# Attention and gated MLP on one core: 64-bit weights made into float32 in place, with other staging and schedule numbers

## The chip, the cores and the metric

The kernel runs on one NeuronCore of one Trainium2 chip. The time is the device time of one execution in microseconds (us); the median of a few runs is compared. The engines named below are PE (matrix products; PEld is its weight load, which overlaps), DVE (vector), ACT (scalar, activations), POOL (general purpose) and SP, which here only issues the DMA transfers. Each engine works through its own instructions strictly in the order in which they were emitted.

## The reference

A causal attention with two kinds of sparse masks (heads 0 to 3 see the last 32 keys, heads 4 to 7 see each 32nd key), then a gated MLP whose gate mixes the 576 positions by a 576x576 matrix:

```python
# B, H, S, D = 8, 8, 576, 64; d_model 512; d_ff 1024
def _attn_ref(q, k, v):
    scores = scale * np.matmul(q, k.transpose(0, 1, 3, 2))
    scores = np.where(masks[None, :, :, :], scores, -1000000000.0)
    scores = scores - np.max(scores, axis=-1, keepdims=True)
    attn = np.exp(scores)
    attn = attn / (np.sum(attn, axis=-1, keepdims=True) + 1e-09)
    return np.matmul(attn, v).astype(np.float32)

def _moe_ref(x, w_in, w_spatial, b_spatial, w_out):
    h = np.maximum(x @ w_in, 0.0)
    u, v = (h[..., :d_ff // 2], h[..., d_ff // 2:])
    mu = np.mean(v, axis=-1, keepdims=True)
    var = np.mean((v - mu) ** 2, axis=-1, keepdims=True)
    v_n = (v - mu) / np.sqrt(var + 1e-06)
    v_s = np.einsum('ts,bsd->btd', w_spatial, v_n) + b_spatial[None, :, None]
    return ((u * v_s) @ w_out).astype(np.float32)
```

`w_in` (512x1024) and `w_out` (512x512) come as 64-bit floats: the input code multiplies a float32 array by a 64-bit scalar. All else is float32.

## The kernel before

**Products.** Every large product is made of three: an operand is split into a rounded part ("0", type fp32r) and the rest ("1"), and the pairs (0,0), (0,1), (1,0) of `PROD` are summed in PSUM. `rnd` makes the rounded part (ACT, DVE or POOL), `rest` the difference (DVE or POOL).

**Stages.** Attention runs per batch and pair of heads `t` (32 of them, four to a batch): scores on PE (L387 local, L497 strided, tiles `s`), masks and maxima (L407 on DVE for local ones; L512 to L525 for strided ones), the exponential on ACT (L424, L530), `normalise` (L360 to L369), a 32x32 transpose on DVE into `pc` (L440, L547), copies of its blocks into `ptl` or `pts` (`rnd`, L318/L320), the products with v (L469, L563, tiles `po`), and the split into `x` (L337 or L339, then L328). The MLP has `moe_1` for a batch (v half L764, u half L806, the mean and variance chain L727 to L751, the split into `vn`), `moe_tail` for the last 64 positions of each batch (same lines, tiles with 64 partitions; its results are `tail` and `tail_b`), and `moe_2`: the spatial product L886 with its last part L898/L899 from the tail, the gate L908, the split into `g`, and the projection L928, whose result goes out through `o`.

**Weights.** Before the first batch can go through the MLP, `weight` has to turn twelve tiles of 128x512 64-bit values (512 KB each) into the two float32 parts: four for the u half of `w_in`, four for its v half, four for `w_out`. A tile is loaded as pairs of 32-bit words into a slot of the rings `u` or `g` (which the MLP itself uses later), two slots each. Then: DVE masks the exponent out of the upper word (L639) into a temporary; ACT turns it into a power of two (L646); DVE extracts the mantissa's upper bits (L652), adds the lower word (L656), POOL or DVE multiplies by the power of two (L660), DVE puts the sign on (L663), and `rnd` and `rest` make the two parts. The temporaries stand in the rings `xt` and `tail`.

**Order.** No order is written out. `Program` collects the operations with what they read and write, a duration on each engine that can do them, and a key; `order` goes through them as a list scheduler would (an idle engine takes the ready operation of the lowest key; an operation with several engines goes to the one that the durations say is done first), and the instructions are emitted in that order. The table `KEYS` holds keys of the first eight attention pairs ("a"), of the weights ("v", "u", "o"), of the spatial weights ("s", "t"), how far ahead attention runs ("lead"), a penalty on DVE ("dp") up to a time ("dpt"), keys of the memsets ("fill") and how far PE looks for a small tiled product beside another ("near"). `warm` puts small products on zeros (L1053) into gaps of PE.

Of the kernel before, what the change touches and what calls it, by code (L numbers as in the profile page):

```python
# [12 lines left out]
U32 = mybir.dt.uint32  # L13
# [66 lines left out]
class Fixed:  # L80
    """A tile that stays; called for it like a Buf."""
# [8 lines left out]
class Buf:  # L90
    """One use of a slot of a ring; its tile is taken from the pool when it is first emitted."""
# [28 lines left out]
class Program:  # L120
    """Operations with what they read and write, put in an issue order for each engine by
    list scheduling: an idle engine takes the ready operation of the lowest key."""

    def __init__(self):
        self.ops, self.writer, self.readers, self.spare = [], {}, {}, {}
        self.tiled = set()

    def add(self, key, choices, fn, reads=(), writes=(), spare=None, tiled=False):
        n = len(self.ops)
        if spare is not None:  # L130
# [23 lines left out]
    def order(self):  # L154
# [12 lines left out]
        issued = []  # L167

# [13 lines left out]
        while len(issued) < len(ops):  # L182
# [45 lines left out]
            taken[n] = True  # L228
            free[e] = now + cost
# [30 lines left out]
def pe_cost(m, n):  # L260
    return max(m / 1.2, n / 2.4 + 3.0)
# [3 lines left out]
def attention_moe(ctx, tc, qT, kT, vl, vs, cst, w_in, w_out, wsp, wtail, out):  # L265
    nc = tc.nc
    nb = qT.shape[0]
    wide = w_in.dtype != F32
# [44 lines left out]
    def rnd(key, n, dst, src, reads, writes, engs=(ACT, DVE, POOL)):  # L313
# [816 lines left out]
```

## Time and profile before

| | |
|---|---|
| runs shown | 564.25, 564.97 (median), 565.13 us |
| span of the profiled execution, first to last instruction | 562.7 us (the page names no other time for it) |
| PE, share of the span | 94% |
| DVE | 64% |
| ACT | 42% |
| POOL | 23% |
| DMA, mean rate over the span | 93 GB/s |
| granted TensorE clock, mean | 0.982 |

How to read it: the shares are averages over two different regimes. The first 100 us make the weights and the attention of the first two batches; the rest is the MLP of eight batches with the attention of the next ones beside it. A row of a group reads: line, engine, operation, output<-inputs, shapes, count | busy us, mean ns of one | idle time before it and what ended most of it. "Busy" counts an instruction from its start to its end, so that two that overlap in the pipe are counted once in a window.

### The profile page before, as it was taken

What the parts mean: (1) busy time and instruction counts of PE and PEld (TensorE: products, weight loads), DVE (VectorE), ACT (ScalarE), POOL (GpSimd) and SP (SyncE); (2) the same over time, 40 slices, a digit from 0 to 9 for tenths busy, and PEclk for the clock granted to TensorE, in tenths of its full rate; (3) what the DMA queues carried; (4) which work ended last, traced back from release to release, by engine and by line L of the source; (5) the groups of instructions that cost most, each with busy time, mean ns of one, the idle gap of its engine ahead of it and who ended that gap; (6) DMA issues with size and microseconds to landing.
All of it is one profiled execution on the core that took longest, in us unless ns stands there. A gap on an engine that the chain in (4) does not pass through costs nothing.

```text
span 562.7 us, 13842 instructions
## 1 busy us (share of the span) xinstructions
PE 529.5 (94%) x5550; PEld 489.4 (87%) x5550; DVE 361.5 (64%) x1090; ACT 236.1 (42%) x733; POOL 129.8 (23%) x200
## 2 busy tenths in 40 slices
PE   7787796899999999999999999999999999999997
PEld 7655676897988989999799989899899989998997
DVE  5799899948488456566836774994645662535232
ACT  7757564714374135333634354571353233212211
POOL 4777987401112022000220121200101010001000
PEclk8999897799999999999999999999999999999999
DMA  7876451416045103035303340461031100010011
GB/s 239 259 226 197 149 205 30 135 44 182 1 144 164 60 24 98 5 120 166 100 1 102 131 129 5 148 183 55 2 104 38 61 31 1 20 46 21 1 43 44
DMA packets 26352, 52.28 MB, mean 93 GB/s; under 512 B 3376, under 2 KB 11696, under 8 KB 26288
## 3 DMA queue, kind: packets, MB, share of 16 engines
q1 hardware_dynamic: 26288, 51.39, 29.8%
q8 instruction: 44, 0.72, 0.6%
q14 instruction: 20, 0.16, 0.1%
HBM read 41.94 MB, written 9.44 MB: 91 GB/s over the span
## 4 chain that ended last, share of the span: by engine, by line
PE 68%; DVE 19%; POOL 4%; ACT 4%; DMA 2%; issue 2%; SPq 0%; POOLq 0%; ACTq 0%; DVEq 0%
PE m L928 17%; PE m L806 15%; PE m L886 14%; PE m L764 13%; ACT pl L424 2%; DVE x L328 2%; PE po L469 2%; POOL ptl L320 2%; PE po L563 2%; PE m L898 1%; PE s L387 1%; PE m L899 1%; DVE bn L732 1%; DVE tail L656 1%; DMA kbd<-kT 1%
## 5 line engine op out<-in xcount | busy, mean ns | idle before, releaser
L886 PE MATMUL m<-wsp_sb,vn 128*128 128x288 f32 x768 | 114.4, 300 | 3.5 <-POOL wsp_sb L328 1.5
L886 PEld LDWEIGHTS m<-wsp_sb,vn 128*128 128x128 f32 x768 | 107.7, 192 | 5.4 <-POOL wsp_sb L328 2.1
L928 PE MATMUL m<-g,w_out_sb 128*128 128x288 f32 x768 | 107.1, 297 | 0.1
L806 PE MATMUL m<-x,w_in_sb 128*128 128x288 f32 x768 | 106.4, 298 | 0.2 <-ACT vv L727 0.2
L806 PEld LDWEIGHTS m<-x,w_in_sb 128*128 128x128 f32 x768 | 104.4, 190 | 1.6 <-ACT vv L727 0.4
L928 PEld LDWEIGHTS m<-g,w_out_sb 128*128 128x128 f32 x768 | 103.5, 188 | 1.5 <-issue 0.8
L764 PE MATMUL m<-w_in_sb,x 128*128 128x512 f32 (+1 forms) x408 | 99.0, 398 | 0.7 <-POOL w_in_sb L328 0.6
L764 PEld LDWEIGHTS m<-w_in_sb,x 128*128 128x128 f32 (+1 forms) x408 | 74.3, 185 | 20.5 <-POOL w_in_sb L328 1.0
L337 ACT COPY o<-m 128x288 f32<-128x288 f32 x55 | 21.9, 399 | 114.4 <-PE m L928 96.6
L908 DVE TENSOR_TENSOR u<-m,u 128x288 f32<-128x288 f32 x64 | 28.4, 454 | 54.5 <-PE m L899 54.1
L328 DVE TENSOR_TENSOR x<-po,x 128x288 fp32r<-128x288 f32 x64 | 35.4, 571 | 39.0 <-ACT x L337 38.5
L744 POOL TENSOR_TENSOR bn<-bn,sel 128x1 f32<-128x1 f32 (+1 forms) x37 | 22.4, 606 | 157.3 <-DVE bn L740 155.5
L424 ACT ACTIVATE pl<-pl,ml 128x64 f32<-128x64 f32 (+1 forms) x160 | 53.6, 337 | 5.5 <-DVE ml L407 5.3
L732 DVE BATCH_NORM_STATS2 bn<-vv 128x6 f32<-128x512 f32 (+1 forms) x37 | 25.4, 687 | 42.0 <-ACT vv L727 41.7
L820 ACT ACTIVATE u<-m 128x288 f32<-128x288 f32 x64 | 25.9, 409 | 44.8 <-PE m L806 44.6
L727 ACT ACTIVATE vv<-m 128x512 f32<-128x512 f32 (+1 forms) x37 | 22.0, 596 | 52.0 <-PE m L764 44.3
L320 POOL TENSOR_SCALAR ptl<-pc 32x320 f32<-32x320 f32 (+3 forms) x67 | 26.4, 394 | 68.1 <-DVE pc L440 34.2
L337 ACT CAST x<-po 128x288 fp32r<-128x288 f32 x59 | 30.0, 543 | 17.9 <-PE po L469 13.1
L751 DVE TENSOR_SCALAR vv<-vv,bn 128x512 f32<-128x512 f32 (+1 forms) x37 | 22.7, 613 | 18.6 <-POOL bn L744 18.5
L424 ACT ACTIVATION_READ_ACCUMULATOR pl<-pl,ml 128x1 f32 (+1 forms) x160 | 30.2, 189 | 0.0
L318 ACT COPY ptl<-pc 32x64 f32<-32x64 f32 (+3 forms) x70 | 24.1, 347 | 14.2 <-DVE pc L440 12.9
L407 DVE CUSTOM_DVE_ANT_0 pl<-s,cst_sb 128x64 f32<-128x64 f32 (+1 forms) x160 | 26.3, 216 | 5.2 <-PE s L387 5.1
(121 smaller groups left out, 666.5 us busy)
## 6 DMA issues: line engine op xcount, KB each, us to landing
q<-qT SPq DMA_DIRECT2D x32, 295.0 KB, 4.8
kbd<-kT SPq DMA_DIRECT2D x64, 144.0 KB, 4.7
outT<-o SPq DMA_DIRECT2D x64, 144.0 KB, 1.8
v_raw<-vs SPq DMA_DIRECT2D x16, 512.0 KB, 3.9
v_raw<-vl SPq DMA_DIRECT2D x16, 384.0 KB, 4.1
u<-w_in SPq DMA_DIRECT2D x4, 512.0 KB, 5.4
g<-w_in SPq DMA_DIRECT2D x4, 512.0 KB, 6.0
g<-w_out SPq DMA_DIRECT2D x4, 512.0 KB, 3.8
```

Of the source, the lines that this page charges most:

```text
L320: eng.tensor_scalar(dst(), src(), 1.0, 0.0, op0=ALU.mult, op1=ALU.add)
L328: eng.tensor_tensor(dst(), src(), f32(hi()), op=ALU.subtract)
L337: eng.copy(dst(), src())
L407: eng.tensor_tensor_reduce(out=p_sb()[:m, u, :], in0=s_ps()[:m, f0 : f0 + 2 * STRIDE], in1=msk[:m], scale=-SCALE, scalar=3.0e38, op0=ALU.a ...
L424: eng.activation(p_sb()[:m, u, :], p_sb()[:m, u, :], AF.Exp, bias=st()[:m, u : u + 1], scale=-1.0, accum_out=st()[:m, NU + u : NU + u + 1],)
L732: lambda eng: eng.bn_stats(bn()[:m, 0:6], v()[:m]), [(v,)], [(bn,)],
L764: eng.matmul(v_ps()[:m, :], x_at(kt)[:, a, :], w_in_sb[:, w, kt, HF:], start=(kt == 0 and i == 0), stop=(kt == NT - 1 and i == 2),)
L806: eng.matmul(u_ps()[:, :HS], w_in_sb[:, w, kt, f * P : (f + 1) * P], xs[NHP * b + kt]()[:, a, r], start=(kt == 0 and i == 0), stop=(kt == ...
L820: lambda eng, u=u, f=f, u_ps=u_ps: eng.activation(u()[:, f * HS : (f + 1) * HS], u_ps()[:, :HS], AF.Relu),
L886: eng.matmul(s_ps()[:, :HS], vn()[:, a, kt, fs], wsp_sb[:, w, kt, r], start=(kt == 0 and i == 0), stop=False,)
L908: lambda eng, ug=ug, s_ps=s_ps: eng.tensor_tensor(ug(), s_ps()[:, :HS], ug(), op=ALU.mult),
L928: eng.matmul(o_ps()[:, :HS], w_out_sb[:, w, f, e * P : (e + 1) * P], g[a]()[:, f, :], start=(f == 0 and i == 0), stop=(f == NT - 1 and i = ...
```

## The change

Four things change together.

1. **`weight`.** The two words of each value are worked on where they lie. The upper word, read as a float32, is multiplied by 2^-112 (which moves its exponent to where the shifted float32 wants it); the lower word is shifted right by 29; the upper word shifted left by 3 is merged into the lower word; and the upper word becomes its own sign merged with that. That is one operation on ACT or DVE and three on DVE, with no temporaries. `rnd` and `rest` then read every second word.
2. **Staging.** The first four tiles are loaded into the one `vn` buffer, which is free until the first batch needs it; the other eight go through `u` and `g` in turn.
3. **Durations in the scheduler.** Several are changed, copies of blocks (`blocks`) and the split of strided `x` (`extra`) get their own, and DVE operations marked `port` are taken to last longer where a marked POOL operation overlaps.
4. **`KEYS`.** Most numbers are different.

```diff
-    "lead": (0.29,),
-    "dp": (1817,),
-    "dpt": (70.0,),
+    "lead": (3.42,),
+    "dp": (1892,),
+    "dpt": (151.06,),
...
+            if n in self.port:
+                if e == POOL:
+                    pool = (now, now + cost)
+                elif e == DVE:
+                    cost += 0.7 * max(0.0, min(pool[1], now + cost) - max(pool[0], now))
...
 def pe_cost(m, n):
-    return max(m / 1.2, n / 2.4 + 3.0)
+    return max(m / 1.2, 4.8 + 0.4464 * n)
...
-        cost = {ACT: 95 + 0.833 * n, DVE: 70 + 0.52 * n, POOL: 110 + 0.833 * n}
+        cost = {ACT: 95 + 0.833 * n, DVE: 70 + 0.52 * n, POOL: 110 + 0.95 * n}
+        if blocks:
+            cost = {ACT: 200 + 0.85 * n, DVE: 175 + 0.5 * n, POOL: 175 + 1.2 * n}
...
-            ba, bb, view2 = temps(tmp)
...
-                    ex_i(), words()[:, :, 1], 0x7FF00000, None, op0=ALU.bitwise_and
...
-                    ex_i(), ex_i(), AF.Relu, bias=sel[:, 2:3], scale=8.0
...
-                    mt_i(), words()[:, :, 1], 0xFFFFF, 0x100000,
...
-                    mt_f(), words()[:, :, 0].bitcast(U32), 2.0**-32, mt_i(),
...
-                    mt_f(), mt_f(), ex_f(), op=ALU.mult
...
-                    mt_i(), words()[:, :, 1], -0x80000000, mt_i(),
...
+            half = lambda j, dt=I32: raw(dt).rearrange("p (n t) -> p n t", t=2)[:, :, j]
+            low, top = (buf, i, 0), (buf, i, 1)
+            val = lambda dt=F32: half(1, dt)
...
+                    eng.activation(val(), val(), AF.Copy, scale=2.0**-112)
...
+                    half(0), half(0), 29, None, op0=ALU.logical_shift_right
...
+                    half(0), half(1), 3, half(0),
+                    op0=ALU.logical_shift_left, op1=ALU.bitwise_or,
...
+                    half(1), half(1), -0x80000000, half(0),
+                    op0=ALU.bitwise_and, op1=ALU.bitwise_or,
...
+        first = r_vn.new()
         for n, job in enumerate(jobs):
-            ring = r_g if n % 2 or n >= 8 else r_u
-            yield job[0], lambda job=job, ring=ring, n=n: weight(*job, ring, n)
+
+            def put(job=job, n=n):
+                stage = (first, n) if n < NT else ((r_g if n % 2 else r_u).new(), 0)
+                weight(*job, stage)
```

What this does to the order of the instructions is seen at three places. The line numbers of the changed kernel are other ones: L635 (scale), L642 (shift), L649 and L657 (merges) take the place of L639 to L663; L338 is the old L328, L330 the old L320, L379 the old L369, L741 the old L744; L479 and L573 are the products with v (old L469, L563), L397 and L507 the scores (old L387, L497).

DVE, some 25 us into the program, around the second and third weight tile; `u_315`, `xt_431` and `vn_101` are weights, `p` and `pc` belong to attention. Before:

```order
L639 TENSOR_SCALAR xt_431<-u_315 128x512
L652 TENSOR_SCALAR xt_431<-u_315 128x512
L512 SCALAR_TENSOR_TENSOR p_81<-s_377,cst_sb 128x288
L547 STREAM_TRANSPOSE pc_443<-pp_70 128x512
L520 TENSOR_REDUCE mx_473<-p_81 128x16
L656 SCALAR_TENSOR_TENSOR xt_431<-u_315,xt_431 128x512
L639 TENSOR_SCALAR tail_487<-g_334 128x512
L652 TENSOR_SCALAR tail_488<-g_334 128x512
```

DVE at the same place now:

```order
L642 TENSOR_SCALAR vn_101<-vn_101 128x512
L530 TENSOR_REDUCE mx_427<-p_81 128x16
L450 STREAM_TRANSPOSE pc_435<-pl_77 128x640
L649 SCALAR_TENSOR_TENSOR vn_101<-vn_101 128x512
L544 TENSOR_REDUCE mx_427<-p_81 128x16
L657 SCALAR_TENSOR_TENSOR vn_101<-vn_101 128x512
```

A tile takes one single-source pass and two merges on DVE where it took two single-source passes, two merges and, for one tile in three, a product.

POOL, in the stretch that ends with the first batch's tail (`tail_1283`, `tail_b_74` from `vv_1168`), for which PE's L898 waits. Before:

```order
L328 TENSOR_TENSOR wsp_sb<-x_372,wsp_sb 128x576
L660 TENSOR_TENSOR xt_1130<-xt_1130 128x512
L369 TENSOR_TENSOR pl_76<-pl_76,ml_78 128x640
L744 TENSOR_TENSOR bn_1182<-bn_1182,sel 64x1
L328 TENSOR_TENSOR w_out_sb<-xt_1130,w_out_sb 128x512
L320 TENSOR_SCALAR ptl<-pc_1224 32x10x32
L320 TENSOR_SCALAR ptl<-pc_1224 32x8x32
L320 TENSOR_SCALAR ptl<-pc_1224 32x4x32
L320 TENSOR_SCALAR ptl<-pc_1224 32x2x32 x2
L320 TENSOR_SCALAR tail_b_74<-vv_1168 64x512
L320 TENSOR_SCALAR w_out_sb<-tail_1193 128x512
L328 TENSOR_TENSOR tail_1283<-vv_1168,tail_1283 64x512
```

POOL at the same place now; the tail's rest stands on DVE (L338, behind the maxima of the next attention pair):

```order
L338 TENSOR_TENSOR wsp_sb<-x_395,wsp_sb 128x576
L330 TENSOR_SCALAR wt_h<-x_396 128x576
L379 TENSOR_TENSOR pl_76<-pl_76,ml_78 128x640
L338 TENSOR_TENSOR w_out_sb<-g_1046,w_out_sb 128x512
L330 TENSOR_SCALAR ptl<-pc_1209 32x10x32
L741 TENSOR_TENSOR bn_1195<-bn_1195,sel 64x1
L330 TENSOR_SCALAR ptl<-pc_1209 32x10x32 x2
L330 TENSOR_SCALAR tail_1261<-vv_1183 64x512
```

The weight product L660 and the rounding of the last `w_out` tile are gone from POOL's work ahead of the tail, the tail's rest has moved to DVE, and the last `w_out` tile is done ahead of the tail's variance chain (L741).

PE, the attention work that stands between the large products in the middle of the program. Before, one of its clusters (`q_2041` and `q_2109` are loaded for the pairs whose scores these are):

```order
L469 MATMUL po_2261<-ptl,v_raw_2012 64x96 x6
L469 MATMUL po_2270<-ptl,v_raw_2012 64x96 x6
L497 MATMUL s_2280<-kbd,q_2041 32x36 x32
L497 MATMUL s_2324<-kbd,q_2109 32x36 x32
L469 MATMUL po_2369<-ptl,v_raw_2082 64x96 x6
L469 MATMUL po_2379<-ptl,v_raw_2082 64x96 x6
```

PE now, one of the clusters, which from here on follow each other about evenly, each with the score and v products of different pairs:

```order
L479 MATMUL po_3352<-ptl,v_raw_2977 64x96 x6
L479 MATMUL po_3360<-ptl,v_raw_2977 64x96 x6
L397 MATMUL s_3371<-kbd,q_2996 32x128 x12
L573 MATMUL po_3389<-pts,v_raw_3046 64x72 x8
L573 MATMUL po_3403<-pts,v_raw_3046 64x72 x8
L397 MATMUL s_3417<-kbd,q_2996 32x128 x6
L507 MATMUL s_3427<-kbd,q_3077 32x36 x32
```

The counts of PE's products are the same in both programs, and PE has done the same work when it comes to the first L898 (now L895).

More of the change, by code (lines that the diff above doesn't have):

```diff
@@ L125, in __init__, with add @@
         self.ops, self.writer, self.readers, self.spare = [], {}, {}, {}
-        self.tiled = set()
-    def add(self, key, choices, fn, reads=(), writes=(), spare=None, tiled=False):
+        self.tiled, self.port = set(), set()
+    def add(self, key, choices, fn, reads=(), writes=(), spare=None, tiled=False, port=False):
         n = len(self.ops)
+        if port:
+            self.port.add(n)
         if spare is not None:
@@ L167, in order @@
         issued = []
+        pool = (0.0, 0.0)
         def release(n):
@@ L311, in attention_moe, with rnd @@
     r_pm = Ring(ps, "m", [P, 512], F32, 4)
-    def rnd(key, n, dst, src, reads, writes, engs=(ACT, DVE, POOL)):
-        cost = {ACT: 95 + 0.833 * n, DVE: 70 + 0.52 * n, POOL: 110 + 0.833 * n}
+    def rnd(key, n, dst, src, reads, writes, engs=(ACT, DVE, POOL), blocks=False):
+        cost = {ACT: 95 + 0.833 * n, DVE: 70 + 0.52 * n, POOL: 110 + 0.95 * n}
+        if blocks:
+            cost = {ACT: 200 + 0.85 * n, DVE: 175 + 0.5 * n, POOL: 175 + 1.2 * n}
         def fn(eng):
@@ L320, in fn, with rest, evac @@
                 eng.tensor_scalar(dst(), src(), 1.0, 0.0, op0=ALU.mult, op1=ALU.add)
-        add(key, [(e, cost[e]) for e in engs], fn, reads, writes)
-    def rest(key, n, dst, src, hi, reads, writes, engs=(DVE, POOL)):
-        cost = {DVE: 70 + 1.04 * n, POOL: 120 + 2.1 * n}
+        add(key, [(e, cost[e]) for e in engs], fn, reads, writes, port=True)
+    def rest(key, n, dst, src, hi, reads, writes, engs=(DVE, POOL), extra=0):
+        cost = {DVE: 70 + 1.04 * n + extra, POOL: 120 + 2.3 * n}
         def fn(eng):
             eng.tensor_tensor(dst(), src(), f32(hi()), op=ALU.subtract)
-        add(key, [(e, cost[e]) for e in engs], fn, reads, writes)
-    def evac(key, n, dst, src, reads, writes, engs=(ACT, DVE)):
-        cost = {ACT: 60 + 0.833 * n, DVE: 70 + 1.04 * n}
+        add(key, [(e, cost[e]) for e in engs], fn, reads, writes, port=POOL in engs)
+    def evac(key, n, dst, src, reads, writes, engs=(ACT, DVE), extra=0):
+        cost = {ACT: 60 + 0.833 * n + extra, DVE: 70 + 1.04 * n + extra}
         def fn(eng):
@@ L371, in normalise @@
             ),
-            [(st, "sum"), *reads], writes,
+            [(st, "sum"), *reads], writes, port=True,
         )
@@ L458, in local_attention @@
                     ],
-                    [(pc,), ("ptl0",)], [("ptl", i, k, c0)],
+                    [(pc,), ("ptl0",)], [("ptl", i, k, c0)], blocks=True,
                 )
@@ L525, in strided_attention @@
             lambda eng: eng.tensor_tensor(view(), view(), each(st()[:, :nu]), op=ALU.subtract),
-            [(st, "max")], [(p_sb,)],
+            [(st, "max")], [(p_sb,)], port=True,
         )
@@ L624, in weight, with scale @@
[L624 to L626 removed]
+    def weight(key, src, n, dst, tok, stage):
+        buf, i = stage
         if src.dtype == F32:
[L628 to L636 removed]
+            val = lambda: buf().bitcast(F32).rearrange(FLAT[len(buf.ring.shape)])[:, 2 * i * n : 2 * i * n + n]
+            load(key - 25, val, src, [(buf, i, 0), (buf, i, 1)], P * n * 4)
+        else:
+            raw = lambda dt: buf().bitcast(dt).rearrange(FLAT[len(buf.ring.shape)])[
+                :, 2 * i * n : 2 * (i + 1) * n
+            ]
+            half = lambda j, dt=I32: raw(dt).rearrange("p (n t) -> p n t", t=2)[:, :, j]
+            low, top = (buf, i, 0), (buf, i, 1)
+            val = lambda dt=F32: half(1, dt)
+            load(key - 25, lambda: raw(I32), src.bitcast(I32), [low, top], P * n * 8)
+            def scale(eng):
+                if hasattr(eng, "activation"):
+                    eng.activation(val(), val(), AF.Copy, scale=2.0**-112)
+                else:
+                    eng.tensor_scalar(val(), val(), 2.0**-112, None, op0=ALU.mult)
+            add(key, [(ACT, 95 + 0.833 * n), (DVE, 70 + 0.52 * n)], scale, [], [top], port=True)
@@ L742, in chain @@
         add(
-            key, [(POOL, 460)],
+            key, [(POOL, 525)],
             lambda eng: eng.tensor_tensor(
@@ L753, in chain @@
             ),
-            [(bn,)], [(v,)],
+            [(bn,)], [(v,)], port=True,
         )
@@ L980, in setup_sel @@
     def setup_sel(eng):
-        for i, v in enumerate((1.0, 0.0, -8.0 * (0x38000000 + (20 << 20)), -0.5)):
+        for i, v in enumerate((1.0, 0.0, 0.0, -0.5)):
             eng.memset(sel[:, i : i + 1], v)
```

93 lines of the change are left out of this document (30 added, 63 removed).

## The prediction

> **What bounds the kernel now.** I read the page first, for where the engines are full.
>
> ```profile
> span 562.7 us, 13842 instructions
> ...
> PE   7787796899999999999999999999999999999997
> ...
> DVE  5799899948488456566836774994645662535232
> ...
> POOL 4777987401112022000220121200101010001000
> PEclk8999897799999999999999999999999999999999
> ```
>
> A slice is 14.1 us. From the eighth slice on PE is full and DVE is not; in the first seven DVE stands at 7 to 9 tenths and POOL at 7 to 9, and PE at 7 or 8 (part of which is products on zeros, L1053). So there are two regimes, and I asked for the busy time of each engine in stretches cut where PE changes (columns: stretch and its length, then PE, PEld, DVE, ACT, POOL with counts, the granted clock, DMA share, GB/s).
>
> ```profile
> 14.00:80.00 66.00, 53.34 (x775) 43.60 (x772) 60.12 (x134) 40.48 (x116) 51.49 (x58) 0.97 0.68 213
> 80.00:102.35 22.35, 14.97 (x154) 12.68 (x152) 20.48 (x60) 14.00 (x51) 18.61 (x19) 0.79 0.23 69
> 102.35:130.00 27.65, 26.96 (x342) 26.12 (x342) 18.09 (x60) 10.72 (x41) 4.29 (x9) 0.92 0.30 89
> 130.00:560.00 430.00, 423.74 (x4160) 397.11 (x4155) 255.72 (x784) 160.83 (x496) 49.41 (x103) 1.00 0.24 71
> ```
>
> Up to 102.35 us DVE is busy 80.6 of 88.35 us (91%), POOL 70.1 (79%), ACT only 54.5. After 102.35 us PE is idle for 0.7 + 6.3 us in 457.65, and for the last 2.7 us of the span, in which the last tile leaves. What comes after 102.35 us can therefore get shorter by 7 us at most; before it there is much more. I put the cut there because of these rows of the timeline (start, duration, engine, line; in brackets idle time before it and who ended it):
>
> ```profile
> 77.37 2.96 PE L764 MATMUL m<-w_in_sb,x 128*64 128x512 f32 x12
> ...
> 90.96 0.68 DVE L732 BATCH_NORM_STATS2 bn<-vv 64x6 f32<-64x512 f32 x1
> ...
> 101.07 1.28 POOL L328 TENSOR_TENSOR tail<-vv,tail 64x512 fp32r<-64x512 f32 x1
> ...
> 102.39 0.61 PE L898 MATMUL m<-wt_h,tail 128*128 128x288 f32 x1 [0.92 <-POOL tail L328]
> ```
>
> PE has the first batch's tail ready at 80.3 us, DVE takes its statistics 10.7 us later, POOL ends its split at 102.35 us. DVE and POOL, with weights and attention queued ahead of the tail, set this moment; call it the **gate**. PE has the same work behind it there in both programs, so the time that the gate moves is the time that the end moves, as long as PE stays full behind it.
>
> **The weights.** Busy time of L639, L652, L656, L663 (all DVE) and L660 (DVE, then POOL) up to the gate, in this order:
>
> ```profile
> 0.00:102.35 102.35, 7.47 (x12) 0.92 0.59 185
> 0.00:102.35 102.35, 8.25 (x12) 0.92 0.59 185
> 0.00:102.35 102.35, 14.29 (x12) 0.92 0.59 185
> 0.00:102.35 102.35, 10.62 (x12) 0.92 0.59 185
> 0.00:102.35 102.35, 4.35 (x4) 10.82 (x8) 0.92 0.59 185
> ```
>
> That is 45.0 us of DVE and 10.8 of POOL. The shift has the form of L639 and L652 (one source in SBUF), the merges that of L656 and L663 (two sources). At the same means the new code takes 13 single-source passes (12 shifts, and one scale that stands on DVE) at 15.72/24 = 0.655 us, and 24 merges at 24.91/24 = 1.038: 8.5 + 24.9 = 33.4 us. DVE **saves 11.6 us**, POOL 10.8. The scale goes to ACT for the other tiles, in place of L646, and ACT, busy 61% of 14 to 80 us, covers it; without that cover the DVE price would be up to 11 more passes, 7.2 us.
>
> These means are far above the shortest ones (ns, min/median/max):
>
> ```profile
> L639 DVE TENSOR_SCALAR xt<-u x4: 404/552/896, 5.2 to 47.5; 128x512 int32<-128x512 int32 x4
> ...
> L656 DVE SCALAR_TENSOR_TENSOR xt<-u,xt x4: 642/860/1704, 6.0 to 50.8; 128x512 f32<-128x512 uint32 x4
> ...
> L663 DVE SCALAR_TENSOR_TENSOR tail<-g,tail x6: 643/713/1101, 24.2 to 97.6; 128x512 int32<-128x512 int32 x6
> ```
>
> With 0.404 and 0.642 the new passes would take 5.3 + 15.4 = 20.7 us. The other 12.7 us are waiting inside the instruction, and the timeline shows on whom: sixteen numbers per partition take 1.23 us, over just the time of POOL's product.
>
> ```profile
> 21.69 1.26 POOL L660 TENSOR_TENSOR tail<-tail,tail 128x512 f32<-128x512 f32 x1
> ...
> 21.76 1.23 DVE L360 TENSOR_SCALAR mx<-mx 128x16 f32<-128x16 f32 x1
> ```
>
> **What is moved between engines.** I counted the rows of both orders up to the tail's split. More on DVE: ten pairs of L407 (one pair per 0.14 us, rows below), two L328 of a strided `x`, one L525 and two L369 of `pp`, one L328 each of `vn`, `wsp_sb` and `tail`, four small L320. Less: two memset pairs.
>
> ```profile
> 98.38 0.21 DVE L407 CUSTOM_DVE_ANT_0 pl<-s,cst_sb 128x64 f32<-128x64 f32 x1
> ...
> 98.52 0.21 DVE L407 CUSTOM_DVE_ANT_0 pl<-s,cst_sb 128x64 f32<-128x64 f32 x1
> ...
> 34.01 0.67 DVE L328 TENSOR_TENSOR x<-po,x 128x288 fp32r<-128x288 f32 x1
> ...
> L369 DVE TENSOR_TENSOR pp<-p,mx 128x288 f32<-128x288 f32 x11 | 5.0, 458 | 0.2
> L328 DVE TENSOR_TENSOR vn<-vv,vn 128x512 fp32r<-128x512 f32 x29 | 20.0, 691 | 0.9 <-ACT vn L318 0.6
> L328 DVE TENSOR_TENSOR wsp_sb<-x,wsp_sb 128x576 fp32r<-128x576 f32 x1 | 1.8, 1840 | 0.0
> L328 DVE TENSOR_TENSOR tail<-vv,tail 64x512 fp32r<-64x512 f32 x7 | 5.4, 772 | 0.2
> L320 DVE TENSOR_SCALAR ptl<-pc 32x64 f32<-32x64 f32 x15 | 3.2, 213 | 0.2
> ```
>
> 1.4 + 1.3 + 1.4 + 0.7 + 1.8 + 0.8 + 0.9 = 8.3, less some 0.3: **8.0 us more**. DVE's net is -3.6 us at unchanged means. POOL loses the eight L660, a split each of `wsp_sb`, `vn` and `tail`, and the three attention products that DVE took; it gains two roundings of `wsp_sb` and six larger copies of blocks for three small ones less.
>
> ```profile
> L328 POOL TENSOR_TENSOR wsp_sb<-x,wsp_sb 128x576 fp32r<-128x576 f32 x3 | 4.8, 1603 | 0.1
> L328 POOL TENSOR_TENSOR vn<-vv,vn 128x512 fp32r<-128x512 f32 x3 | 4.7, 1567 | 0.0
> L369 POOL TENSOR_TENSOR pp<-p,mx 128x288 f32<-128x288 f32 x5 | 3.8, 756 | 10.5 <-ACT pl L424 10.4
> L320 POOL TENSOR_SCALAR wsp_sb<-x 128x576 fp32r<-128x576 f32 x1 | 0.7, 671 | 0.0
> L320 POOL TENSOR_SCALAR ptl<-pc 32x320 f32<-32x320 f32 x20 | 11.5, 577 | 64.7 <-DVE pc L440 34.2 <-PE po L469 17.2 <-DVE ml L407 4.7
> ```
>
> 10.8 + 1.6 + 1.6 + 1.3 + 3 x 0.76 = 17.6 less; 2 x 0.67 and, for the copies, some 3 us more (an estimate: six at 0.577 less small change): about **13 us less** of its 70, 18%. If DVE's waiting goes with it, the 12.7 us above and about as much again in other short operations such as L360 lose 18%, some 4 us. DVE is then 7.5 us shorter, and of its 7.75 us of idle time before the gate I give back 1.5, since fewer of its steps wait for POOL. **The gate moves by -9 us**, to about 93. Bounds: -2 (3.6 us, with new stalls in the strict order) and -15 (rival (a)).
>
> Two waits are new. On DVE the first merge L649 waits for ACT's scale, with the maxima L407 queued behind it, for which PE's fillers and ACT's exponentials wait; the merge before L663 waited in the same place for POOL, so I cost it at nothing, between -1 and +1 us. And ACT clears `ptl` ahead of the first scale, which POOL did (some 1 us): the merges then end near 8.5 us, when the first scores come. On SP's queue the last `w_out` load no longer waits for a slot freed late, and nothing is moved behind a later wait; nothing counted.
>
> **Behind the gate.** PE's idle time shows in stretches where local attention and the MLP meet:
>
> ```profile
> 153.00:176.00 23.00, 21.33 (x381) 18.80 (x381) 18.42 (x78) 16.03 (x63) 5.33 (x12) 1.00 0.33 98
> ...
> 348.00:370.00 22.00, 20.55 (x364) 18.72 (x362) 18.27 (x60) 12.45 (x43) 4.12 (x9) 1.00 0.38 104
> ```
>
> 1.7 and 1.5 us, with DVE at 80%. The new order spreads attention evenly, so I give **-2 us** of the 7; bounds -6 and +5, the loss if the splits of `g` that now stand on POOL (about 0.75 us each, estimated from the split of `wsp_sb` by its size, against 0.45 on DVE) or single pairs late in the program make PE wait.
>
> **Sum.** 562.7 - 9 - 2 = 551.7 us of span. The median of the runs stands 564.97 - 562.7 = 2.3 us above the profiled span, which I take over: **554 us**.
>
> **Rivals.** (a) *One port, used in turn.* DVE's waits above are as long as POOL's instruction, so DVE and POOL may go through this stretch as one resource. Then POOL's whole 13 us count, and DVE's saving at its shortest times (11 single-source passes and four products less, at 0.404 and 0.642 us: 7.0), less some 5 us moved onto DVE: -15 us at the gate, **548 us**. [...] I give it 0.17: much of DVE's work here reads PSUM or one tile and runs beside POOL. (b) *Another chain holds the gate.* The tail still has to pass L732, POOL's power, L751 and the split behind attention in strict order, and the spatial weights on POOL now come in one bunch; the gate then moves by 3 us and the rest by nothing: **562 us**, 0.17. (c) *Slower: passes that write every second word.* All three DVE passes now write with a step of two words, which no row shows. Rows with wide steps are dear: a strided `x` takes 0.67 us (34.01, above) where a contiguous one takes
>
> ```profile
> 23.66 0.41 DVE L328 TENSOR_TENSOR x<-po,x 128x288 fp32r<-128x288 f32 x1
> ```
>
> 0.41. At that factor of 1.63 the merges cost 24 x 0.40 and the single passes 13 x 0.25 us more, 12.9 us: the gate moves by +4, the end to 567, and with DVE's delay lengthening POOL's waits some **569 us**. It decides from about 11 us of added DVE time, 0.3 us on each pass. Against it: L639 reads with this very step at 0.404 us. [...] No run here shows the write. I give it 0.08. (d) *The schedule gives it back:* the gate moves, but PE waits as much more behind it, 564 to 566 us: 0.04.
>
> **How the numbers follow.** The forecast (549.5 to 560) has 0.54. A measurement of this kernel tells 0.2% (1.1 us) from no change. Faster by more: forecast, (a) and (b), 0.88. Slower by more: (c) and a quarter of (d), 0.09; the rest of (d), 0.03, lies within it. The range reaches from (a) to (b), 546 to 562.5 us.
>
> **What would show it.** DVE passes of the new lines at 0.4 and 0.65 us where POOL is idle, with means below 0.66 and 1.04; DVE busy about 73 us from 14 us to the gate; the first L895 near 93 us; less than 5 us of PE idle time behind it. Wrong: merges of 1 us with POOL idle (c); an L895 still near 100 us with DVE idle before it (b); or a gate at 93 and an end above 555 (d).

## The result, and the profile after

The changed kernel takes **545.12 us** (median of 4 runs, 544.18 to 546.24) against 565.05 us of the kernel before on the same chip (4 runs, 564.25 to 565.35): a ratio of 0.9649, 95% interval 0.9625 to 0.9673. It is 19.9 us faster, about twice the 11 us that were forecast, and 0.9 us below the low end of the range. The profiled execution is the run of 544.18 us.

The page of the changed kernel, the same lines as of before:

```profile
span 541.7 us, 13802 instructions
...
PE   6989969999999999999999999999999999999997
...
DVE  4899999457156767576583866656555271436232
...
PEclk9899979999999999999999999999999999999999
```

A slice is now 13.5 us. PE stands at 8 or 9 tenths from the second slice to the fifth and is full from the seventh on, with one gap, in the sixth; DVE still stands at 8 or 9 up to the seventh. The stretches up to the gate (here PE's first L895, at 88.65 us) and behind it, with the same columns as before:

```profile
14.00:88.65 74.65, 65.82 (x928) 55.32 (x928) 69.57 (x178) 50.09 (x149) 57.30 (x65) 0.93 0.66 212
88.65:130.00 41.35, 40.83 (x507) 37.02 (x508) 25.85 (x110) 26.22 (x95) 22.64 (x40) 1.00 0.42 129
130.00:541.70 411.70, 407.67 (x3990) 384.12 (x3989) 227.69 (x682) 154.96 (x465) 59.24 (x116) 1.00 0.22 68
```

and of the kernel before the last stretch, to the end of its span:

```profile
130.00:562.70 432.70, 423.74 (x4160) 397.11 (x4155) 255.72 (x784) 160.83 (x496) 49.41 (x103) 1.00 0.24 71
```

**The 21.0 us of span come from two places.** The gate moves from 102.39 to 88.65 us, -13.7: between 14 us and the gate DVE's busy time falls from 80.6 to 69.6 us (-11.0) and its idle time from 7.75 to 5.1 us (-2.7). What lies behind the gate shrinks from 460.3 to 453.05 us, -7.3: PE's idle time there from 9.65 to 4.55 us (-5.1), its busy time from 450.7 to 448.5 us (-2.2).

The conversion of the weights on DVE up to the gate: the one scale on DVE (L637), the shift (L642) and the two merges (L649, L657):

```profile
0.00:88.65 88.65, 0.63 (x1) 0.94 0.68 214
...
0.00:88.65 88.65, 7.42 (x12) 0.94 0.68 214
...
0.00:88.65 88.65, 10.13 (x12) 0.94 0.68 214
...
0.00:88.65 88.65, 10.27 (x12) 0.94 0.68 214
```

28.45 us for 37 passes, against 45.0 us for 52 before. Their single times, from the views of these lines (ns, shortest, median, longest):

```profile
L642 DVE TENSOR_SCALAR vn<-vn x4: 416/423/523, 5.1 to 27.8; 128x512 int32<-128x512 int32 x4
L642 DVE TENSOR_SCALAR u<-u x4: 413/691/1530, 31.0 to 67.6; 128x512 int32<-128x512 int32 x4
L642 DVE TENSOR_SCALAR g<-g x4: 410/540/901, 32.4 to 74.7; 128x512 int32<-128x512 int32 x4
...
L657 DVE SCALAR_TENSOR_TENSOR u<-u x4: 673/1058/1782, 37.5 to 68.9; 128x512 int32<-128x512 int32 x4
L657 DVE SCALAR_TENSOR_TENSOR g<-g x4: 627/712/1025, 38.1 to 77.1; 128x512 int32<-128x512 int32 x4
```

The shortest (0.410 and 0.627 us) are about those of the old passes (0.404 and 0.642 us): writing every second word costs nothing that shows here. Medians and longest times still lie above them, most of all for the tiles in `u`.

The last thing to see is where PE's full stretch starts. PE's timeline ahead of the gate:

```profile
68.79 1.29 PE L397 MATMUL s<-kbd,q 128*32 128x128 f32 x36
74.30 2.19 PE L573 MATMUL po<-pts,v_raw 128*64 128x72 f32 x32 [4.22 <-issue]
76.42 4.60 PE L761 MATMUL m<-w_in_sb,x 128*64 128x512 f32 x12
80.85 6.56 PE L883 MATMUL m<-wsp_sb,vn 128*128 128x288 f32 x48
87.34 1.29 PE L397 MATMUL s<-kbd,q 128*32 128x128 f32 x36
88.65 0.40 PE L895 MATMUL m<-wt_h,tail 128*128 128x288 f32 x1
```

The tail no longer makes PE wait: PE arrives at the first L895 out of full work, and its last long wait ends at 74.30 us. DVE's and ACT's rows say on what:

```profile
71.26 2.34 DVE L338 TENSOR_TENSOR wsp_sb<-x,wsp_sb 128x576 fp32r<-128x576 f32 x2 [0.56 <-POOL wsp_sb L330]
73.52 1.27 DVE L338 TENSOR_TENSOR x<-po,x 128x288 fp32r<-128x288 f32 x2
...
72.54 1.17 ACT L347 CAST x<-po 128x288 fp32r<-128x288 f32 x2 [0.81 <-ACT pl L434]
```

The ring `x` has eight slots, in which attention outputs and the spatial weights' staging take turns. I read the rows so: ACT's evacuation L347 stands idle until DVE has split the spatial weight whose slot it takes (the first of the two splits ends just before 72.54 us; the step of ACT named in the bracket had ended earlier); DVE's L338 on `x` follows, then PE gets its `po` bank. No run frees that slot alone.

### The profile page after: what moved, and what is told of

Read it like the earlier page. It is cut to its first block, busy times and chain, and to the rows that moved or that the text cites. A ratio compares the mean times of both kernels' runs of the same rounds, so it can differ in the third digit from the quotient of the medians.

```text
span 541.7 us, 13802 instructions
## 1 busy us (share of the span) xinstructions
PE 523.0 (97%) x5546; PEld 484.5 (89%) x5546; DVE 329.6 (61%) x1023; ACT 242.9 (45%) x743; POOL 144.3 (27%) x233
## 4 chain that ended last, share of the span: by engine, by line
PE 87%; POOL 4%; DVE 3%; DMA 3%; ACT 2%; issue 1%; SPq 0%; POOLq 0%; DVEq 0%; ACTq 0%
PE m L925 19%; PE m L761 18%; PE m L883 18%; PE m L803 17%; PE po L479 3%; PE s L397 3%; PE po L573 3%; DMA kbd<-kT 3%; PE s L507 2%; PE m L895 2%; PE m L896 2%; PE po L1050 1%; PE m L1050 1%; POOL ptl L330 1%; ACT pl L434 1%
## 5 line engine op out<-in xcount | busy, mean ns | idle before, releaser
L883 PE MATMUL m<-wsp_sb,vn 128*128 128x288 f32 x768 | 111.8, 296 | 0.0
L883 PEld LDWEIGHTS m<-wsp_sb,vn 128*128 128x128 f32 x768 | 105.5, 189 | 0.9
L761 PE MATMUL m<-w_in_sb,x 128*128 128x512 f32 (+1 forms) x408 | 100.9, 403 | 0.8 <-issue 0.8
L347 ACT COPY o<-m 128x288 f32<-128x288 f32 x61 | 24.1, 398 | 87.9 <-PE m L925 76.8
L741 POOL TENSOR_TENSOR bn<-bn,sel 128x1 f32<-128x1 f32 (+1 forms) x37 | 21.5, 583 | 156.5 <-DVE bn L737 156.2
L338 DVE TENSOR_TENSOR x<-po,x 128x288 fp32r<-128x288 f32 x64 | 34.8, 575 | 30.8 <-ACT x L347 30.5
L347 ACT CAST x<-po 128x288 fp32r<-128x288 f32 x56 | 28.5, 547 | 50.7 <-PE po L479 38.4
L330 POOL TENSOR_SCALAR ptl<-pc 32x64 f32<-32x64 f32 (+3 forms) x76 | 30.8, 406 | 58.0 <-PE po L479 43.5
L330 POOL TENSOR_SCALAR pts<-pc 32x288 f32<-32x288 f32 x26 | 12.3, 475 | 83.7 <-PE po L573 75.8
L748 DVE TENSOR_SCALAR vv<-vv,bn 128x512 f32<-128x512 f32 (+1 forms) x37 | 20.6, 558 | 21.6 <-POOL bn L741 21.5
L328 ACT COPY ptl<-pc 32x320 f32<-32x320 f32 (+3 forms) x75 | 25.9, 345 | 8.8 <-DVE pc L450 4.4
```

What stands on the lines that cost most here:

```text
L328: eng.copy(dst(), src())
L330: eng.tensor_scalar(dst(), src(), 1.0, 0.0, op0=ALU.mult, op1=ALU.add)
L338: eng.tensor_tensor(dst(), src(), f32(hi()), op=ALU.subtract)
L347: eng.copy(dst(), src())
L761: eng.matmul(v_ps()[:m, :], x_at(kt)[:, a, :], w_in_sb[:, w, kt, HF:], start=(kt == 0 and i == 0), stop=(kt == NT - 1 and i == 2),)
L883: eng.matmul(s_ps()[:, :HS], vn()[:, a, kt, fs], wsp_sb[:, w, kt, r], start=(kt == 0 and i == 0), stop=False,)
```

## The experiments

Ends are medians. "Gate" and "behind" (span less gate) are of each profiled run. Where another order puts more or fewer products ahead of the gate than the 876 of both kernels, "even" reckons the gate, and the behind column with it, for the same products as there. Nearly all that differ are attention's small ones, and they are priced by kind, from the changed kernel's groups behind its gate: 0.040 us for a local score (14.5 us for 360), 0.013 for a strided score (10.1 for 768), 0.051 and 0.038 for a local and a strided product with v (16.0 for 312, 14.7 for 384), 0.29 for a product with the tail (18.7 for 64). The profiled run can lie some way off the median (561.56 against 558.48 us in e5, 559.35 against 560.84 in e13), so 2 or 3 us in these columns decide nothing.

### Which part makes the gain

Three parts of the diff can be had apart: the conversion (`weight`), the staging (`put`: four weights in `vn`, the others through `u` and `g` in turn, where before all went through `u` and `g` and the last four through `g`), and the numbers for the scheduler (keys, durations, port rule).

**e1, conversion and staging; e2, numbers alone.** e1 is the changed kernel with these taken back, e2 the kernel before with these put in:

```diff
-    "a": (-614.2, -120.8, -119.9, -106.1, 434.1, -10.4, -9.8, 205.1,),
+    "a": (-550.4, -120.8, -119.9, -93.3, 467.8, -10.4, -3.9, 240.8,),
...
-        if port:
-            self.port.add(n)
...
-    return max(m / 1.2, 4.8 + 0.4464 * n)
+    return max(m / 1.2, n / 2.4 + 3.0)
```

> The new conversion and staging alone, with the old keys, durations and no port rule in the scheduler. Theory 1 (the conversion sets the gate through the sum of DVE's instructions, waiting included; the scheduler's numbers set what lies behind the gate): DVE's conversion near 28.5 us up to the gate, first L895 near 92 us, time behind the gate near 460 us, end near 554 us. Theory 2 (the scheduler's numbers do most of both): gate near 100 us, end 560 us or more.

> The new keys, durations and port rule alone, with the old conversion and staging. Theory 1: first spatial product of the tail stays near 100 to 102 us, time behind the gate falls to about 453 us, end near 556 us. Theory 2: gate at 95 us or earlier, end 549 us or less.

e1: 565.27 us, ratio 0.9998 (0.9980 to 1.0016). e2: 565.98 us, 1.0014 (0.9991 to 1.0037). **Neither half alone gives anything.** Theory 1 fell in both; theory 2 has the end of e1, and fell in e2. In e1 the gate stands at 95.66 us, but with 104 products fewer ahead of it (72 local scores and 32 products with v, 4.1 us): even, it moves by 2.6 us only, and what lies behind it gets 5.7 us longer. PE and ACT in e1:

```profile
75.84 8.15 PE L799 MATMUL m<-x,w_in_sb 128*128 128x288 f32 x48 [8.06 <-ACT u L813]
...
83.13 1.02 ACT L813 ACTIVATE u<-m 128x288 f32<-128x288 f32 x3 [1.97 <-POOL w_out_sb L334]
```

PE waits 8.1 us for the MLP's `u`: ACT's L813 comes, in ACT's order, behind attention steps that wait for DVE (1.66 us ahead of the copy of `pts` at 72.86 us), and the next one waits 2.0 us more until POOL has split a `w_out` tile that is staged in `u`.

**e3, e4: conversion and staging with the durations and port rule, or with the keys.**

> The new conversion and staging with the new durations and port rule, but the old keys. Theory 1: gate near 90 us (as with the conversion alone, within 2), time behind the gate 455 to 460 us, end near 548 to 552 us. Theory 2: if the keys are the part of the schedule that counts, gate near 98 us and end near 558 us; if the durations are, as the changed kernel, 545 us.

> The new conversion and staging with the new keys, but the old durations and no port rule. Theory 1: gate near 90 us, time behind it 455 to 460 us, end near 548 to 552 us. Theory 2: if the durations are the part that counts, gate near 98 us and end near 558 us; if the keys are, as the changed kernel, 545 us.

e3: 556.04 us, 0.9838 (0.9808 to 0.9868), between what the two theories had. e4: 550.88 us, 0.9752 (0.9717 to 0.9787), as theory 1 had it for the end and the time behind (456.6 us), though with its gate at 95.29 us and not near 90. The keys are worth 14.4 us on top of e1, the durations 9.2, both 20.2.

**e5, conversion alone, with the old staging; e6, the changed kernel with the old staging.** The same edit to e1 and to the changed kernel:

```diff
-        first = r_vn.new()
...
-                stage = (first, n) if n < NT else ((r_g if n % 2 else r_u).new(), 0)
+                stage = ((r_g if n % 2 or n >= 8 else r_u).new(), 0)
```

> The new conversion alone, with the old staging too (weights through u and g, the last four through g), old keys, old durations. The conversion with the new staging alone ended where the kernel before does. Theory S (staging: weights that now pass through u late hold up the MLP's u, and cost what the shorter conversion gains): gate near 93 us, end near 556 us. Theory F (fit: the issue order comes out of keys that were set for the longer conversion, and DVE's saved time turns into waits in that order, whatever the staging): end within 4 us of 565, PE idle or filled before the gate as much as in the kernel before, 41 us of both.

> The changed kernel with the old staging. Theory S: new keys and durations with the old staging keep most of the gain, end 545 to 549 us. Theory F: any other list of operations under the same keys loses part of the gain, end 550 us or more.

e5: 558.48 us, 0.9902 (0.9872 to 0.9933): the conversion by itself is worth **6.0 us** (564.52 us before on that chip), between theory S (near 556 us) and F (561 or more). e6: 554.93 us, 0.9831 (0.9816 to 0.9845), a loss as theory F had it, and its trace shows where. The staging costs 6.8 us under the old numbers (e5 to e1) and is worth 9.8 us under the new ones (e6 to the changed kernel). What it does there begins on SP's queue. The last `w_out` load, in the changed kernel and in e6:

```profile
60.26 0.39 SPq L354 DMA_DIRECT2D g<-w_out  x1
```

```profile
76.48 0.33 SPq L354 DMA_DIRECT2D g<-w_out  x1
```

(in the kernel before: 79.20 us). Four tiles one after the other in the two slots of `g` make the last one late; its last merge on DVE starts at 87.7 us, while the tail is being made, where in the changed kernel it starts at 77.1. The merges from `g`, PE's timeline and its stretches in e6:

```profile
L657 DVE SCALAR_TENSOR_TENSOR g<-g x8: 650/710/1815, 20.9 to 87.7; 128x512 int32<-128x512 int32 x8
```

```profile
89.83 0.61 PE L894 MATMUL m<-wt_h,tail 128*128 128x288 f32 x1 [6.64 <-POOL tail L338]
```

```profile
83.00:89.80 6.80, 0.20 (x8) 0.05 (x2) 4.57 (x25) 4.47 (x12) 5.03 (x8) 0.87 0.51 146
89.80:95.00 5.20, 5.17 (x47) 4.37 (x48) 4.09 (x30) 5.09 (x28) 5.00 (x7) 0.51 0.01 2
```

PE idles 6.6 us for the tail, then runs 5.2 us at half the clock. The late tile's own merges do not hold the tail up, since they start at 86.96 and 87.67 us, behind DVE's last step for it (86.50); DVE only reaches the tail's statistics at 82.02 us, and POOL its power at 85.92, behind copies for attention. Most of the loss lies behind the gate: of the 11.9 us between the two spans, 2.7 are at the gate (even), some 2.5 are the clock, and some 7 lie between 117 and 128 us, where PE waits for the next attention's keys and maxima and fills in with products on zeros. Those keys are loaded behind eight result stores in SP's order; in the changed kernel four of the eight come ahead of the next loads and the rest between them. The stores in e6, the wait, and the four in the changed kernel:

```profile
98.10 17.86 SPq L943 DMA_DIRECT2D outT<-o  x8
```

```profile
122.80 0.86 PE L397 MATMUL s<-kbd,q 128*32 128x128 f32 x24 [2.46 <-DMA kbd<-kT]
```

```profile
96.66 3.52 SPq L944 DMA_DIRECT2D outT<-o  x4
```

That this order of loads and stores is the cause was not tried by itself.

**e13, the old conversion under the new staging and numbers.** e2, with the old `weight` reading from the new stages.

> The old conversion under the new staging, keys, durations and port rule. Theory P (the parts work only together; the shorter conversion is what the new order feeds on): gate at 99 us or later, end 562 us or more. Theory Q (staging and numbers do most of it by themselves, and the numbers alone failed only for want of the staging): gate near 93 us, end 552 us or less.

560.84 us, 0.9921 (0.9891 to 0.9951): between the theories, nearer to P. Its stretches up to and behind its gate:

```profile
14.00:105.57 91.57, 70.68 (x941) 58.45 (x941) 78.88 (x200) 56.23 (x169) 74.32 (x80) 0.89 0.57 176
105.57:130.00 24.43, 24.43 (x339) 23.52 (x338) 14.69 (x51) 14.62 (x53) 13.21 (x23) 1.00 0.41 130
130.00:557.40 427.40, 423.63 (x4149) 396.99 (x4147) 240.00 (x735) 163.99 (x495) 63.46 (x122) 1.00 0.23 70
```

Behind the gate it stands as well as the changed kernel (451.8 us); all that is missing is ahead of it. The seven together:

| kernel | end | gate | products ahead | gate, even | behind, even |
|---|---|---|---|---|---|
| before | 565.05 | 102.39 | 876 | 102.4 | 460.3 |
| e5 conversion | 558.48 | 95.27 | 925 | 94.8 | 465.0 |
| e1 conversion, staging | 565.27 | 95.66 | 772 | 99.8 | 466.0 |
| e2 numbers | 565.98 | 101.34 | 876 | 101.3 | 462.9 |
| e13 staging, numbers | 560.84 | 105.57 | 889 | 104.7 | 452.7 |
| e6 conversion, numbers | 554.93 | 89.83 | 840 | 91.3 | 462.3 |
| changed: all three | 545.12 | 88.65 | 876 | 88.7 | 453.0 |

The last columns read plainly: **staging with numbers gives what is gained behind the gate (-7.6 us in e13, -7.3 in the changed kernel), and the conversion gives what is gained at the gate (-16 us from e13 to the changed kernel)**. Each needs the rest: under the old numbers the conversion gives back behind the gate part of what it gains ahead of it (e5), and with the new staging more than all of it (e1); without the new staging the numbers gain nothing behind it (e2, e6). The new staging alone was not run.

### What a microsecond of DVE is worth in a kept order

These keep every engine's order as it is, and change only what an instruction does.

**e7: the kernel before, without the merge of the sign.** **e8: the changed kernel, without its first merge.**

```diff
-                ({DVE: 1.04}, [(buf,)], lambda eng: eng.scalar_tensor_tensor(
-                    mt_i(), words()[:, :, 1], -0x80000000, mt_i(),
-                    op0=ALU.bitwise_and, op1=ALU.bitwise_or,
-                )),
+                ({DVE: 1.04}, [(buf,)], lambda eng: None),
```

```diff
-                lambda eng: eng.scalar_tensor_tensor(
-                    half(0), half(1), 3, half(0),
-                    op0=ALU.logical_shift_left, op1=ALU.bitwise_or,
-                ),
+                lambda eng: None,
```

> The kernel before with the order of every engine kept, but without the merge that puts the sign back (the weights lose their sign): 12 two-source passes of DVE less, 10.6 us at their mean and 7.7 us at their shortest. If the gate hangs on DVE's sum in the order as it stands (the prediction's term): gate 7 to 10 us earlier, end near 555 to 558 us. Theory F: half of it or less shows at the gate, since POOL, ACT or a load ends the next wait in the same order: gate 0 to 5 us earlier, end 560 us or more.

> The changed kernel with the order of every engine kept, but without the first merge (the weights lose their lowest bits): 12 two-source passes of DVE less, 10.1 us at their mean and 7.7 us at their shortest. If the gate hangs on DVE's sum: gate 7 to 10 us earlier, end near 536 to 538 us. Theory F: the order was fitted with these passes in it, and other waits take over: gate 0 to 5 us earlier, end 540 us or more.

e7: 559.60 us (before 564.52), ratio 0.9905 (0.9888 to 0.9922), gate 96.97, between the two theories. e8: 542.70 us, 0.9615 (0.9601 to 0.9630), gate 86.87, as theory F had it.

**e9: one more shift, by nothing. e14: also each first merge made twice** (the same bits again, so the weights stay). e14 has 61 conversion passes on DVE up to the gate where the old program has 52; they take 43.0 us, nearly the old program's 45.0, in the new order.

```diff
-                lambda eng: eng.tensor_scalar(
-                    half(0), half(0), 29, None, op0=ALU.logical_shift_right
+                lambda eng: (
+                    eng.tensor_scalar(half(0), half(0), 29, None, op0=ALU.logical_shift_right),
+                    eng.tensor_scalar(half(0), half(0), 0, None, op0=ALU.logical_shift_right),
```

> The changed kernel with the order of every engine kept, and a second shift of DVE, by nothing, behind the first: 12 one-source passes more, 7.4 us at their mean and 4.9 us at their shortest. In this order 9.8 us less of DVE moved the gate by only 1.8 us. Theory K (the kept order has little slack on DVE, and a second chain just behind it): added DVE time shows at the gate by half or more, gate 2.5 to 7 us later, end 548 to 553 us. Theory L (a load or another engine holds the gate, and DVE has slack): gate 0 to 2 us later, end 547 us or less.

> The changed kernel with the order of every engine kept, each shift followed by a shift by nothing and each first merge made twice: 12 one-source and 12 two-source passes more, 17.6 us of DVE at their means and 12.8 us at their shortest. The 12 one-source passes alone moved the gate by 8.5 us and the end by 7.3 us. Theory P: the second dozen costs as much per us of DVE again, gate near 105 to 108 us, end 561 to 565 us, all of the gain gone. Theory Q: end 556 us or less, the order keeps half of its gain under the longer conversion.

e9: 552.45 us, 0.9778 (0.9759 to 0.9797), theory K in its end, though the gate moves by 8.5 us, more than it had. e14: 557.34 us, 0.9850 (0.9820 to 0.9881), between P and Q. The stretch up to the gate in e8, in e9 and in e14:

```profile
14.00:86.87 72.87, 63.23 (x929) 53.30 (x929) 60.67 (x171) 50.30 (x153) 54.39 (x65) 0.98 0.72 222
```

```profile
14.00:97.14 83.14, 67.79 (x928) 56.90 (x928) 75.06 (x189) 50.64 (x151) 57.07 (x65) 0.92 0.62 195
```

```profile
14.00:101.89 87.89, 67.77 (x928) 55.87 (x928) 82.57 (x200) 50.50 (x152) 59.37 (x65) 0.90 0.59 184
```

**e10: POOL's subtractions for the weights' low parts become clears. e12: two passes in place of three ahead of the tail.**

```diff
+            if clear and eng is nc.gpsimd:
+                eng.memset(f32(dst()), 0.0)
+                return
```

```diff
-            eng.tensor_tensor(raw(0), raw(1), f32(wt_b), op=ALU.subtract)
-            eng.tensor_scalar(raw(0), raw(0), sel[:, 0:1], None, op0=ALU.mult)
+            eng.tensor_scalar(raw(0), raw(1), sel[:, 0:1], None, op0=ALU.mult)
...
-        for i, v in enumerate((1.0, 0.0, 0.0, -0.5)):
+        for i, v in enumerate((1.0, -1.0, 0.0, -0.5)):
```

> The changed kernel with the order of every engine kept, and the subtractions of the weights' low parts that stand on GpSimd replaced by clears of one source less (the weights lose these low parts). One port used in turn: DVE's passes, now 28.5 us of conversion up to the gate against 20.7 at their shortest, lose most of the 7.8 us of waiting, and the gate moves 4 us or more, end 541 us or less. Theory K: DVE's waiting shrinks, but as with the merge taken out the gate moves by 2 us at most, end 542.5 us or more.

> A version that may be faster: the changed kernel in its kept order, with the choice between a row of the tail's weights and its remainder made in two DVE passes in place of three (one of 1.8 us less, 10 us ahead of the gate). If DVE's chain into the tail holds the gate: gate 1 to 2 us earlier, end near 543.5 us. If another chain stands beside it, as the run without the merge suggests: 0 to 0.8 us, 544.3 to 545.1 us.

e10: 542.91 us, 0.9609 (0.9592 to 0.9625), theory K. e12: 545.06 us, 0.9650 (0.9635 to 0.9665): nothing gained, so DVE's chain into the tail no longer holds the gate. The stretch up to the gate in e10:

```profile
14.00:87.69 73.69, 64.37 (x928) 54.84 (x928) 64.81 (x180) 51.15 (x156) 46.51 (x67) 0.95 0.68 216
```

Together, DVE and POOL as busy time from the start to the gate, all against the kernel whose order they keep (end: 564.52 us for e7, 545.12 us for the others):

| run | DVE | POOL | gate | end | behind the gate |
|---|---|---|---|---|---|
| e7, order of before | -7.8 | -3.3 | -5.4 | -4.9 | 462.1 |
| e8 | -9.8 | -3.7 | -1.8 | -2.4 | 453.1 |
| e10 | -4.8 | -11.9 | -1.0 | -2.2 | 452.9 |
| e9 | +6.0 | -0.6 | +8.5 | +7.3 | 454.2 |
| e14 | +14.1 | +1.6 | +13.2 | +12.2 | 453.1 |

Three things follow. With the changed kernel's order kept, the time behind the gate stays at 453 to 454 us whatever happens ahead of it, so the gate's move is the end's move, as the prediction had it. **DVE time that is added shows in full (0.9 us for each in e14, 1.4 in e9); DVE time that is taken away shows by 0.7 in the order of before and by 0.2 in the new one**: the changed kernel stands at the bend, with the wait of 74.30 us (73.05 in e8) close behind DVE's sum. And e14 still beats the kernel before by 7.8 us with its DVE passes as long as the old ones. Its gate, at 101.89 us, is within 0.5 us of the old one, so that gain lies behind the gate, as in e13; POOL's freed time shows little at the gate there.

### Is it any change of order

**e11: one number of the scheduler, `near`, taken back. e15: a version that might be faster**, e12's edit with the first two spatial weights' keys lower by 200.

```diff
-    "near": (69.95,),
+    "near": (41.5,),
```

```diff
-    "s": (661.1, 498.1, 943.5, 820.7,),
+    "s": (461.1, 298.1, 943.5, 820.7,),
```

> The changed kernel with one number of the scheduler taken back, near, from 69.95 to 41.5; every instruction stays, only the order differs. Theory F (the time hangs on how well the order fits the list of operations): 3 us or more slower than the changed kernel, 548 us or more. Theory C (the conversion makes the gain and the order is of second rank): within 1.5 us of the changed kernel, 544 to 546.7 us.

> A version that may be faster: two passes in place of three for the tail's weights (worth nothing by itself), and the keys of the first two spatial weights lower by 200, so that their staging leaves its slot before the attention output that waits for it. In the changed kernel PE idles 4.2 us at 70 us, behind that output. If this wait is what PE's full stretch starts with: idle time there under 2 us, end 541.5 to 543.5 us. If another wait stands beside it (the load of keys, the maxima): 544.5 to 546 us.

e11: 545.32 us, 0.9654 (0.9638 to 0.9669), the same as the changed kernel, although some 160 of DVE's 1000 rows stand elsewhere. So it isn't that every other order is worse. But up to the gate DVE's 231 rows stand in the same order but for one, and nearly all that moves lies behind it, where PE is full: e11 says nothing of the order ahead of the gate. e15, which does change it: 551.81 us, 0.9750 (0.9723 to 0.9777), 6.7 us slower. PE's waits ahead of its gate:

```profile
67.49 8.18 PE L802 MATMUL m<-x,w_in_sb 128*128 128x288 f32 x48 [2.05 <-ACT u L816]
80.28 4.20 PE L760 MATMUL m<-w_in_sb,x 128*64 128x512 f32 x12 [2.25 <-ACT u L816]
93.50 0.40 PE L894 MATMUL m<-wt_h,tail 128*128 128x288 f32 x1
```

The wait of 4.2 us at the attention output is gone, and two waits of 2 us for the MLP's `u` have come, with the gate 5 us later. Whether freeing that slot alone would be worth something isn't settled by it, since the order changed with the keys; freeing it in the kept order wasn't tried. No version that beats the changed kernel was found.

## Why the prediction was right or wrong

**Right: direction, regimes, mechanism at the gate.** The time falls, PE is full behind the gate and DVE with POOL set it, the conversion is what moves it (e13 to the changed kernel, e14). POOL lost 12.8 us up to the gate (13 forecast), the passes at a step of two words cost what the old ones did (0.410 and 0.627 us at their shortest, against 0.404 and 0.642), and with the changed kernel's order kept the end moves as the gate does.

**The gate's term was too small: -9 forecast, -13.7 measured.** Its steps: DVE -3.6 us at unchanged means, and "some 4 us" of waiting less, 18% of what I took DVE to wait. Measured is -11.0 us of DVE (-11.5 from the start of the program), and -2.7 us of idle time where 1.5 were given. All DVE work but the conversion grew by 5.0 us, about what the moved steps with their share of less waiting came to; it is the conversion's waiting that was mis-sized. The passes took 28.45 us where their means gave 33.4: over their shortest times they waited 7.8 us, not 12.7, so the waiting fell by 39%, not by POOL's 18%. e10 gives the price that I should have looked for: 11.9 us of POOL's subtractions less took 4.8 us off DVE, 0.4 us for each. POOL's 12.8 us less come to 5.1 us by it, so 3.6 + 5.1 = 8.7 of the 11.0 us are accounted for, and the other 2.3 stay open. The eight products L660 may have stood right beside the conversion's own passes, but the rows at 21.69 and 21.76 us show it for a small attention step only, and no run takes these products out of the kernel before.

**The term behind the gate failed in size, and in one step.** I gave -2 with a bound of -6; measured is -7.3. Idle time gives -5.1, within the bound. The idle time that went lies partly where the prediction looked for it, where attention meets the MLP (L563), and partly at the tails (L898). PE's longest waits behind the gate, before, and the longest one now:

```profile
PE m L898 <- DVE tail L328: 1.6, 2, 1.0
PE po L563 <- POOL bn L744: 1.2, 1, 1.2
PE m L898 <- POOL tail L328: 0.9, 1, 0.9
```

```profile
PE m L925 <- POOL g L338: 0.5, 1, 0.5
```

The other -2.2 is the clock, which the prediction did not count: "PE has the same work behind it there in both programs, so the time that the gate moves is the time that the end moves, as long as PE stays full behind it." The work is the same and PE is nearly full, but its clock is not the same. Of the kernel before, then of the changed kernel:

```profile
96.00:102.35 6.35, 2.50 (x52) 1.93 (x46) 6.32 (x32) 6.23 (x28) 5.82 (x9) 0.80 0.54 159
102.35:106.00 3.65, 3.60 (x26) 3.33 (x28) 2.96 (x11) 2.18 (x12) 1.70 (x2) 0.50 0.57 164
106.00:112.00 6.00, 6.00 (x50) 5.81 (x48) 5.92 (x27) 3.73 (x15) 1.20 (x3) 0.95 0.39 115
```

```profile
70.10:74.30 4.20, 0.00 (x1) 0.03 (x1) 3.64 (x5) 2.76 (x10) 4.20 (x5) 0.86 0.50 144
74.30:78.00 3.70, 3.70 (x36) 2.93 (x37) 3.68 (x6) 3.51 (x8) 3.70 (x4) 0.50 0.14 16
```

Before, PE ran 3.65 us at half clock just behind the gate, and 6 us at 0.95: 3.65 x 0.5 + 6 x 0.05 = 2.1 us lost. In the changed kernel its last half-clock stretch ends ahead of the gate (0.50 up to 79 us, 1.00 from 80 us on). The gaps of 4.2 us here and of 6.6 us in e6 are followed by half clock. In the kernel before, so is the longest gap ahead of the gate, 2.98 us (to 99.43 us; 0.50 from 100 to 106 us), and one of 2.72 us (to 61.63 us; 0.50 from 63 to 65 us), while behind one of 2.68 us (to 56.80 us) the granted clock is 1.00. No run varies the length of a gap alone.

**The step that was left at nothing: the staging.** "On SP's queue the last `w_out` load no longer waits for a slot freed late ...; nothing counted." e6 shows that it is worth 9.8 us under the new numbers, most of it behind the gate, through the clock after a longer wait for the tail and through attention that comes late there; e13 shows that staging and numbers together carry all the gain behind the gate. The prediction put that gain down to attention spread evenly and gave it 2 us.

**The rivals.** (a) came nearest in time (548), and its -15 us nearest at the gate, but the runs do not bear out its mechanism: of the 11.9 us that e10 takes off POOL only 4.8 reach DVE's busy time, and of the 7.8 us that the passes waited 3.1 go. The gate, which moved by 1.0 in e10, can't tell, since in this order little of any DVE time taken away shows there (e8). What is borne out is its direction: DVE's passes shorten when POOL does less, by these 3.1 us, and 2.2 us of the 4.8 reach e10's end. (b) fell: the gate moved by more than the forecast. (c) fell by the rows of L642 and L657. (d) is wrong for the whole change, for which I had priced it; in e1 the schedule does give it all back, in e5 in part.

**The range** reached down to (a) at the gate with the middle value behind it. The two bounds that the text itself gives, -15 and -6, add up to 562.7 - 15 - 6 + 2.3 = 544.0 us, and that end would have held the result.

## What to carry to other kernels

In a program whose order comes out of a list scheduler, the worth of a shorter operation isn't a property of the operation: here the same conversion was worth 6 us under the old numbers and staging, 11 us under the new numbers with the old staging (e2 to e6), and 15.7 us with both new (e13 to the changed kernel), while conversion and new staging together under the old numbers gave nothing. Forecast a change of code and of schedule as one, look first at what the new order does to the loads and to the chain that ends at the gate, and let the range take the far ends of its terms together. To price one operation by itself, keep the order and change what the instruction does: adding and taking away tell on which side of the bend the kernel stands.

## What the runs showed of the hardware

Long waits of PE cost more than themselves here. Behind the 4.2 us gap PE ran 3.7 us at a granted clock of 0.50, behind e6's 6.6 us gap 5.2 us at 0.51: 1.9 and 2.5 us more, in the stretch that follows; a granted clock of 0.50 also followed gaps of 2.72 and 2.98 us in the kernel before, but not one of 2.68 us there. And POOL's work lengthened DVE's by a part, not by its whole: in e10 4.8 us less for 11.9 us less of POOL, 0.4 us for each, while DVE's single passes range from 0.41 to 1.53 us for one and the same shift.
